# A transformer block on one core: the second feed-forward block by seven sums, the first one as jobs of the order list, key and value rows by column groups, key sums in pairs

## The chip, the cores and the metric

The kernel runs on one core of a Trainium2 chip. The metric is the device time of one execution in microseconds (us). The engines are TensorE (PE, matrix products; PEld is its weight load), VectorE (DVE), ScalarE (ACT), GpSimd (POOL) and SyncE (SP), whose queue issues nearly all DMAs. Each engine takes its instructions in the order in which the program hands them out and waits on semaphores for the others.

## The reference

```python
x = A_x                                        # 1 x 2048 x 576, bf16
sa, ca, ga, sb, cb, gb = split(silu(c) @ w_mod, 6)
h = layernorm(x) * (1 + ca) + sa
q, k, v = heads(h @ wqkv)                      # 32 heads of 18
pq, pk = q @ w_phi, k @ w_phi                  # per head
phi = concat(softmax(p), softmax(-p))          # for pq and for pk
o = (phi_q @ (phi_k^T v)) / (phi_q . sum(phi_k) + 1e-6)
x = x + ga * (o @ wo)
h = layernorm(x) * (1 + cb) + sb
x = x + gb * (relu(h @ w1) @ w2)               # 576 -> 4608 -> 576
```

## The kernel before

The 2048 tokens are 16 tiles of 128. The attention runs over all tiles first, and the feed-forward layers then run over eight blocks of two tiles (256 tokens).

**The order list.** The first part is written out by hand as the string `ORDER`, a list of jobs. A job name stands for a function, the number behind it for a tile or part, and the number after the colon for the pair of PSUM banks that its product goes to (four pairs; pair 3 is taken by the key-value sum while that runs). A job's instructions are handed out when its word comes up, so the list fixes each engine's order, but not what engines do relative to each other: there, data and buffers decide.

The jobs that the texts speak of:

- `FK`, `FQ`: the key and query weights are folded with `w_phi` on PE; `fra`/`frd` and `FQra`/`FQrd` copy the result from PSUM on ACT or DVE. `sc`, `sh`, `m2` are products for the modulation (`m2c` are the copies behind `m2`); `Z` and the spins in `sc`/`sh` are products of zeros.
- `KR`, `VR`, `QR` work out four correction rows of the folded weights. They let the layer norm's mean and shift ride along as four additional rows of x. Those rows of x come from `sa`/`sp` (statistics), `T` (transpose) and `Tc` (copy). `xd`, `xa`, `xp` scale x on DVE, ACT or POOL.
- `K`, `Q`, `V` project one tile (ten products of 288 columns, L282). `eK`/`eQ` take the exponents on ACT, `sK` and `qs` sum them on DVE, `rK` takes the reciprocals by Ln and Exp on ACT, `pA`, `pM`, `qp` scale on POOL, `vE` scales v on DVE out of PSUM. `kv` adds a tile to the key-value sum; `kv0` is the first of the sixteen, `kz` masks the result.
- `qt` transposes a query tile by DMA, `nu` is the attention product, `nO` its division on DVE, `ot`/`oc` the transpose, `W` the output product, `xr` the residual, `lb` the statistics, `ap` the normalisation, `ht`, `hd`, `ha` the transpose and modulation of block 0's input. `wo` scales the output weights on POOL.
- `td`: part of `t_part`, the differences T1 to T4 of quarters of the second feed-forward weights that the second layer works with (DVE, 128x1728 each, 12 in all).

**The feed-forward blocks.** After the list a loop runs over the eight blocks. `l2` is the second layer: seven products of quarters with sums between them, in place of eight. The first layer has two forms. `l1` is the plain one: nine groups of two column blocks, 36 products of 64 rows each, two beside each other (L732). `l1_seven` does the same by seven products out of sums, in the order written out in `SEVEN` (L781 and L798). Blocks 0 and 1 use `l1`, blocks 2 to 7 `l1_seven`:

```python
BS = 2
for b in range(NB):
    if b < BS:
        l1(b, ...)
    else:
        l1_seven(b, in_seven(b))
    l2(b, in_l2(b))
    if b + 2 < NB:
        project(2 * b + 4, WO)
```

The seven products need sums of quarters of the first layer's weights, made once by `w1_sum(k, gp)` with k from 0 to 3, for two halves gp of the columns, each 128x2048, in place. They read further quarters that `w1_more` loads. Sums k = 2 and 3 overwrite what `l1` reads. `t_feat` makes the sums of the block's input. Before, the sums lie in hooks of blocks 0 and 1: k = 0, 2, 3 on DVE and k = 1 on POOL in pieces of 512 columns:

```python
o, p, q, op = ((f[6], v[0], v[6], ALU.subtract), (f[7], v[7], f[6], ALU.subtract),
               (f[1], v[1], f[7], ALU.subtract), (f[2], v[2], v[3], ALU.add))[k]
eng.tensor_tensor(out=o, in0=p, in1=q, op=op)
```

Block 0's attention for tiles 2 and 3, the T differences and the loads also lie in hooks of blocks 0 and 1.

Of the kernel before, what the change touches and what calls it, by code (L numbers as in the profile page):

```python
# [7 lines left out]
P = 128  # L8
# [10 lines left out]
NC = 5  # L19
# [26 lines left out]
Lbdw Z11 LwkT FK Z1 fra1 Lx0 Lcc sx bn0 sd frd2 Lwsc frd0 bn1 sa0 frr sc ca Lwsh frd4 Lx2 Lid bn3 sh fra3 sp0 T0:1 shc  # L46
Lt0 KR:2 KRh0 Lwv Lx4 xd0 bn2 KRh1 mk KRd0 KRd1 Tc0 sa2 Ka0:0 VR:1 bn4 VRh0 Kb0 VRd0 sp2 VRh1 Lt1 xd2 Ka1:2 Kb1 VRd1
T2:1 eKa0 sK0 LwqT FQ3:3 Tc2 K2:0 FQra3 bn5 Lwsb eKa1 sK1 K3:3 rK0 eK2 sa4 FQ4:2 FQrd4 pM0 V0:1 sK2 Lwcb rK1 pA1 pA0
Lt2 pM1 V1:0 m2:2 eK3 FQ0:3 Lx6 vE0 V2:1 Lwga vE1 rK2 Lx10 m2c FQrd0 pA2 FQ1:3 xa4 sp4 Lt4 bn7 vE2 T4:2 Tc4 K4:0 FQra1
eK4 FQ2:2 xp6 bn6 sa6 FQrd2 sK3 Lt3 bn11 K5:1 pM2 kv0 kv1 QR:2 eK5 V3:0 kv2 QRh sp6 QRe QRd T6:2 rK3 sK4 pA3 vE3 rp  # L50
Tc6 pM3 K7:1 rK4 K6:2 pM4 pA4 eK7 eK6 Lwgb ga:0 gac V4:1 bn9 kv3 sK5 rK5 bn8 pA5 w2b0 sa8 V5:2 vE4 bn12 sp8 T8:0 xa8
pM5 vE5 Tc8 Q0:1 eQ0 gb:2 xp14 kv4 kv5 sK6 bn10 Q1:0 gbc sa10 sK7 gaw gar wl1 rK6 K8:1 qs0 wl3 bn15 eQ1 eK8 K9:2 eK9
sp10 xp10 Lwo Q2:0 pA6 sK8 pM6 eQ2 V6:1 rK8 bn13 vE6 sK9 bn14 qp0 rK7 Q3:2 pA8 T10:0 Tc10 pA7 eQ3 qs1 pM7 kv6 K10:1
eK10 rK9 K11:0 sK10 pM8 V8:2 eK11 sa14 sa12 V7:1 vE8 pM9 rK10 V9:0 vE7 xa12 sp12 pA9 kv7 T12:2 sK11 rK11 kv8 V10:1 vE9
kv9 wl0 pA10 vE10 Tc12 pM10 K12:0 sp14 T14:2 Tc14 gbw eK12 kv10 K13:1 eK13 wo2 K14:2 eK14 qt0 qs2 sK12 sK13 Q4:0 eQ4
rK13 K15:1 w2a1 qp1 V11:2 V12:0 gbr qs3 wo1 pA11 qp2 pM11 vE11 kv11 w2a2 rK12 w2a0 pA12 eK15 vE12 sK15 pM12 qt1 V13:2
kv12 pM13 Lmask sK14 Q5:1 wl4 rK15 eQ5 sq5 Q6:0 pA13 pA15 vE13 sq4 kv13 qt2 V15:2 rK14 vE15 pM15 pA14 V14:1 vE14 eQ6
Q11:2 pM14 qp3 sq6 kv14 kv15 qt3 eQ11 sq11 Q7:1 kz nu1:2 Q8:0 nu0:3 nO1 td2 eQ7 eQ8 sq7 nO0 td0 sq8 ot1:2 td1 Q9:1 oc1
Q10:0 ot0:2 wo0 wo4 eQ9 qi5 wo3 sq9 oc0 eQ10 W1:3 xr1 qi4 W0:1 lb1 Q12:2 xr0 lb0 Q13:0 lr1 eQ12 sq10 qi6 lr0 ap1 eQ13
Q14:1 ht1:2 Q15:3 ap0 wl2 ht0:0 ha eQ14 eQ15 hd w2b1 sq13 sq15 sq14 sq12  # L60
# [16 lines left out]
BS = 2  # L77
# [4 lines left out]
def tile_block(ctx, tc, a, out):  # L82
# [60 lines left out]
    m98 = carve(RS, NC * GR, (NC, NX))  # L143
    rep = carve(RS, NC * GR + NC * NX, (NC, 32))
# [13 lines left out]
    rs2 = small([P, NT, 2], FP32, "rs2")  # L158
    Rq = small([P, 2, 2 * H], FP32, "Rq")
# [90 lines left out]
    def mods(w, bank, idle=None):  # L250

        o = PS[:, bank, :] if isinstance(bank, int) else bank[:, 0, :]
        for k, wm in enumerate(w):
            for ci in range(NC):
                if idle is not None:
                    spin(1, idle)
# [16 lines left out]
    def rows_mm(raw, pr):  # L273
        for k in range(2):
            for ck in range(NC):
                pe.matmul(pr[0:NX, k, 0:HD], lhsT=m98[0:R, ck, :], rhs=raw[0:R, ck, k * HD:(k + 1) * HD],  # L276
                          start=(ck == 0), stop=(ck == NC - 1))

# [14 lines left out]

    def hs(r, s):
        return r.rearrange("p (h s) -> p h s", s=2)[:, :, s]
# [5 lines left out]
    def vv(t):  # L301
        return v_sb[:, (t + 1) % NV, :].rearrange("p (h e) -> p h e", e=VW)
# [4 lines left out]
    def k_r(t):  # L307
        Rr, r = Rk[:, t % 4, :], rk[:, t % 4, :]
# [18 lines left out]
    def kv(t):  # L327
        E = E_sb[:, t % NE, :]
        for c in range(9):
            k, o, n = kvcols(c)  # L330
            pe.matmul(PS[:, 6 + k, o:o + n], lhsT=E[:, c * P:(c + 1) * P],  # L331
                      rhs=v_sb[:, (t + 1) % NV, KVC[c][0] * VW:KVC[c][0] * VW + n],
# [23 lines left out]
    def eslot(u):  # L356
        return u % NET if u < 8 else u % 2
# [185 lines left out]
    def scale():  # L543
        dve.tensor_scalar(out=ca1[0:R, :], in0=PS[0:R, 7, 0:NC], scalar1=1.0, scalar2=None, op0=ALU.add)
        dve.tensor_scalar(out=m98[0:R, :, X0:X0 + 3], in0=ca1[0:R, :].unsqueeze(2).to_broadcast([R, NC, 3]), scalar1=-1.0,
                          scalar2=None, op0=ALU.mult)

    def x_scale(t, eng):
# [6 lines left out]
        for ck in range(NC):  # L555
# [76 lines left out]

    def stats_p(t):
        c = sc[:, t % 4:t % 4 + 2, :]
        pool.tensor_copy(c[:, :, X0:X0 + 2], mv[:, 0, t:t + 2, 0:1].to_broadcast([P, 2, 2]))
        pool.tensor_tensor(out=c[:, :, X0 + 2], in0=mv[:, 0, t:t + 2, 0], in1=c[:, :, X0], op=ALU.subtract)
        pool.tensor_scalar(out=rs[:, t:t + 2, 1], in0=rs[:, t:t + 2, 0], scalar1=-1.0, scalar2=None, op0=ALU.mult)

    def k_scale(t):
        pool.tensor_scalar(out=Ak[:, t % 4, :], in0=hs(rk[:, t % 4, :], 0), scalar1=rs[:, t, 0:1], scalar2=None, op0=ALU.mult)  # L640

    def k_minus(t):
        Rr, r = Rk[:, t % 4, :], rk[:, t % 4, :]
        pool.tensor_copy(vv(t)[:, :, DH], hs(r, 0))
        pool.tensor_tensor(out=rat[:, t % 4, :], in0=hs(Rr, 0), in1=hs(r, 1), op=ALU.mult)
# [11 lines left out]
        "sc": lambda: mods([wsc], 7, idle=6),  # L657
        "sh": lambda: mods([wsh], 7, idle=6),
        "shc": lambda: dve.tensor_copy(m98[0:R, :, X0 + 3], PS[0:R, 7, 0:NC]),
# [3 lines left out]
        "rp": lambda: pool.tensor_copy(rep[0:R], siluc[0:R, :].unsqueeze(2).to_broadcast([R, NC, 32])),  # L663
        "xd": lambda t: x_scale(t, dve), "xp": lambda t: x_scale(t, pool), "xa": lambda t: x_scale(t, act),
# [5 lines left out]
        "sK": k_sums, "rK": k_r, "pA": k_scale, "pM": k_minus,  # L670
# [17 lines left out]
        "td": lambda k: t_part(0, k, dve),  # L688
# [3 lines left out]
    for w in "KV":  # L692
        JOBS[w + "R"] = lambda w=w: rows_mm(ROWS[w], at[w + "R", None])
        for k in range(2):
            JOBS[f"{w}Rh{k}"] = lambda w=w, k=k: rows_h(at[w + "R", None], k)
# [512 lines left out]
```

## Time and profile before

| what | value |
|---|---|
| time, median of 3 runs | 374.89 us (374.74 to 375.1) |
| the profiled execution | 374.84 us, span 373.1 us |
| granted TensorE clock | 1.0 |
| busy: PE, DVE, ACT, POOL | 99%, 76%, 59%, 37% of the span |
| first key-value product (`kv0`) | 30.15 us |
| block 0's first layer from / second from | 90.7 / 112.1 us |
| block 1's first layer from / second from | 130.7 / 148.4 us |
| block 2's first layer from / second from | 167.0 / 183.2 us |

The span is what the profiler records from first to last instruction; the time holds 1.74 us more. Waits before a matrix product show as gaps in the chain of waits. A "busy" engine of DVE or POOL may contain waiting inside an instruction, which shows as an instruction that takes longer than others of its form.

### The profile page before, as it was taken

The page shows a single profiled execution, that of the slowest core. Times are in us where ns is not written, and L with a number is a line of the kernel's source. Part 1 is how long each engine was busy: PE and PEld are TensorE (multiplying, and loading weights), DVE is VectorE, ACT ScalarE, POOL GpSimd, SP SyncE. Part 2 cuts the span into 40 slices and gives each one's busy share as a digit, 9 for nine tenths or more (in the row PEclk, how much of TensorE's full clock was granted, in tenths as well). Part 3 has the DMA queues.
Part 4 walks back from the last instruction along what each step waited for, and adds up shares of the span by engine and source line. Part 5 has one row for each costly group of instructions (what it writes and reads, how often), then busy time and mean ns, then how long its engine had stood idle before and what let it go on. Part 6 is the DMA issues. An engine that isn't in the chain of part 4 may idle for free.

```text
span 373.1 us, 14298 instructions
## 1 busy us (share of the span) xinstructions
PE 367.7 (99%) x6245; PEld 313.6 (84%) x6245; DVE 282.4 (76%) x508; ACT 220.0 (59%) x495; POOL 138.9 (37%) x203
## 2 busy tenths in 40 slices
PE   8999999999999999999999999999999999999996
PEld 4787888888888788889988987898799889979975
DVE  2999998679979779987795688578668747745752
ACT  2598998588633435608752774478167608844730
POOL 2167999840302567380054007102600240044023
DMA  8985799887966436463127236512521123101001
GB/s 296 414 362 154 271 411 315 218 238 296 265 187 132 125 81 152 126 133 95 36 46 182 35 35 83 147 37 52 128 52 20 37 50 37 35 0 36 4 2 33
DMA packets 58591, 49.96 MB, mean 134 GB/s; under 512 B 46880, under 2 KB 50848, under 8 KB 57760
## 3 DMA queue, kind: packets, MB, share of 16 engines
q1 hardware_dynamic: 58384, 48.88, 48.1%
q8 instruction: 49, 0.80, 0.9%
q10 hardware_dynamic: 144, 0.16, 0.1%
q14 instruction: 14, 0.11, 0.1%
HBM read 31.98 MB, written 5.90 MB: 102 GB/s over the span
## 4 chain that ended last, share of the span: by engine, by line
PE 96%; DVE 1%; ACT 1%; issue 0%; POOL 0%; DVEq 0%; POOLq 0%
PE PS L878 33%; PE PS L798 23%; PE PS L282 15%; PE PS L732 10%; PE PS L946 4%; PE PS L781 3%; PE PS L401 2%; PE PS L331 2%; PE PS L238 1%; PE PS L276 1%; PE PS L953 1%; PE PS L418 1%; PE PS L918 1%; ACT R L558 1%; DVE RH L459 0%; DVE st L243 0%
## 5 line engine op out<-in xcount | busy, mean ns | idle before, releaser
L878 PEld LDWEIGHTS <-RH 128*128 128x128 f16 x846 | 81.7, 98 | 21.2 <-issue 0.4
L866 POOL TENSOR_TENSOR yt<-yt,gb_row 128x288 f32<-128x288 f32 x23 | 27.5, 1194 | 176.1 <-DVE yt L865 176.1
L798 PEld LDWEIGHTS <-R 64*128 64x128 bf16 (+1 forms) x1824 | 76.0, 94 | 0.8 <-issue 0.2
L878 PE MATMUL PS<-R,RH 128*128 128x288 bf16 (+1 forms) x558 | 73.2, 286 | 0.0
L798 PE MATMUL PS<-h,R 64*128 64x128 bf16 x1056 | 69.2, 216 | 0.0
L828 ACT ACTIVATE RH<-PS 128x512 f16<-128x512 f32 x96 | 50.9, 605 | 9.2 <-PE PS L798 9.0
L798 PE MATMUL PS<-RE,R 64*128 64x128 f16 x768 | 48.1, 216 | 0.0
L287 ACT ACTIVATE RT<-PS,rs 128x576 bf16<-128x576 f32 x64 | 42.9, 744 | 3.6 <-PE PS L282 3.4
L878 PE MATMUL PS<-RT,RH 128*128 128x288 f16 x288 | 37.9, 286 | 0.0
L732 PE MATMUL PS<-h,R 64*128 64x256 bf16 (+1 forms) x684 | 36.3, 264 | 0.0
L732 PEld LDWEIGHTS <-R 64*128 64x128 bf16 x684 | 31.6, 94 | 3.9 <-issue 0.2
L975 ACT ACTIVATE h<-h,mod 128x256 bf16<-128x256 bf16 x63 | 32.5, 589 | 1.0 <-DMA h<-xn 1.0
L282 PE MATMUL PS<-RH,R 116*128 116x288 bf16 x240 | 32.7, 286 | 0.1
L798 PE MATMUL PS<-h,early 64*128 64x128 bf16 x384 | 32.0, 216 | 0.0
L282 PE MATMUL PS<-RH,RT 116*128 116x288 bf16 x240 | 31.5, 286 | 0.0
L818 ACT ACTIVATE yt<-PS 128x512 f32<-128x512 f32 x10 | 6.0, 597 | 42.7 <-PE PS L798 41.8
L243 DVE BATCH_NORM_STATS2 st<-x_sb 128x6 f32<-128x288 bf16 x64 | 25.7, 443 | 6.3 <-DMA x_sb<-in_xk_dram 6.2
L865 DVE TENSOR_TENSOR yt<-PS,RS 128x288 f32<-128x288 f32 x23 | 10.5, 456 | 23.4 <-PE PS L878 23.3
L282 PEld LDWEIGHTS <-R 116*128 116x128 bf16 x240 | 22.6, 98 | 6.2 <-ACT R L626 0.4
L282 PEld LDWEIGHTS <-RT 116*128 116x128 bf16 x240 | 22.9, 98 | 5.5
L798 PEld LDWEIGHTS <-w 64*128 64x128 f16 (+1 forms) x480 | 26.4, 94 | 0.0
L867 POOL TENSOR_TENSOR x_sb<-yt,x_sb 128x288 bf16<-128x288 f32 x30 | 24.9, 833 | 3.5 <-DVE yt L863 1.7
(153 smaller groups left out, 737.9 us busy)
## 6 DMA issues: line engine op xcount, KB each, us to landing
R<-in_w_dram SPq DMA_DIRECT2D x4, 1152.0 KB
eqd<-RT SPq DMA_DIRECT2D x12, 288.0 KB, 3.6
RT<-eqd SPq DMA_DIRECT2D x12, 288.0 KB, 3.1
R<-in_w2b_dram SPq DMA_DIRECT2D x2, 1296.0 KB, 6.7
R<-in_w2a_dram SPq DMA_DIRECT2D x3, 864.0 KB
out_dram<-x_sb SPq DMA_DIRECT2D x15, 144.0 KB, 1.8
RT<-in_xT_dram SPq DMA_DIRECT2D x2, 640.0 KB, 6.5
x_sb<-in_xk_dram SPq DMA_DIRECT2D x8, 144.0 KB, 3.6
```

What stands on the lines that cost most here:

```text
L243: dve.bn_stats(out=s[:, hf, :], in_=x_sb[:, t % 8 if n else t, hf * HD:(hf + 1) * HD])
L282: pe.matmul(pr[:, k, 0:HD], lhsT=xt(t, ck), rhs=w[0:R, ck, k * HD:(k + 1) * HD], start=(ck == 0), stop=(ck == NC - 1))
L287: act.activation(out=E.rearrange("p (b h s e) -> p b h s e", b=2, s=2, e=DH)[:, :, :, s, :], in_=pr[:, :, 0:HD].rearrange("p b (h e) -> p ...
L732: pe.matmul(PS[:, 2 * u + hf, n * 256 + o:n * 256 + o + w], lhsT=w1_lhs(hf, c, j, h), rhs=hb[b0:b0 + 64, c, o:o + w], start=(n == 0 and c ...
L781: pe.matmul(PS[:, bank_at[n], j * 256:j * 256 + 256], lhsT=w1_lhs(hi, c, j, hi), rhs=hb[64 * hi:64 * hi + 64, c, :], start=(j == 0 and c = ...
L798: pe.matmul(PS[:, bank_at[BK[n] + str(g)], i * P:(i + 1) * P], lhsT=w[r, (4 * c + i) * P:(4 * c + i + 1) * P], rhs=x, start=(n in ("M1", " ...
L828: act.activation(out=o, in_=v[{"k11": "Y", "k12": "Z", "k21": "X", "k22": "W"}[n]], func=ACT.Relu)
L866: pool.tensor_tensor(out=y, in0=y, in1=gb_row[:, c], op=ALU.mult)
L867: eng.tensor_tensor(out=xs(t)[:, c], in0=y, in1=xs(t)[:, c], op=ALU.add)
L878: pe.matmul(PS[:, bank, 0:HD], lhsT=am[:, j, :], rhs=bm[:, j, :], start=first and j == 0, stop=(j % 9 == 8), skip_group_check=True)
L946: pe.matmul(pr[:, k, 0:HD], lhsT=oT[:, t % 2, ci, :], rhs=wo_sb[:, ci, k * HD:(k + 1) * HD], start=(ci == 0), stop=False, skip_group_check ...
L975: act.activation(out=o, in_=o, func=ACT.Identity, scale=mod(1, c), bias=mod(0, c))
```

## The change

- `BS` becomes 1: only block 0 uses the plain first layer, block 1 uses `l1_seven`.
- Block 0's first and second layer become jobs of the list: `lm` (a group of the first layer), `lu` (its ReLU, two on ACT and one on DVE), `lv` (U2 = U3 + A22 on DVE), `pa` (half a product of the second layer), `pc` (copy on ACT), `pf` (finish: DVE, then POOL), `px`/`py` (sums on DVE), `po` (store). So do `ou`, `wf`, `wr`, `xR` (tiles 2 and 3), the T differences `tb`, `tc`, `te` on DVE (`tep`: on POOL), the loads `wm`, and `w1_sum` as `ws` (on POOL, 2048 columns in one instruction) and `wt` (on DVE). The number behind `ws`, `wt`, `wm` is 2k + gp. In the list are `ws0` to `ws3` and `ws7`, `wt4` to `wt6`, `te1`, `te2` and `tep0`.
- The key and value rows are worked out by column groups (`quarters`, four groups of 144 columns on 32 columns of the array), as the query rows were. The value rows then go through four small DMAs, as the query rows did.
- The list sums keys in pairs: `rK`, `pA` and the new `pR` work on two tiles at once, `T`, `Tc`, `sa`, `sp` on four from tile 4 on.
- All five `FQ` copies are on ACT, x of tiles 0 and 1 is scaled by DVE (three chunks) and ACT (two), the value buffers are numbered anew, tiles 2 and 3 are normalised on ACT (`aP`), the spins within `sc` and `sh` become four ahead of `sc`. The order of loads and of the list's jobs is new throughout.

The diff, cut to its core:

```diff
@@ ORDER, from the last kv products to the end (new)
+sq4 pM15 vE15 kv14 qi5 kv15 Q6:0 qt1 kz nu1:3 eQ6 qt3 nu0:2 Q11:1 nO1 ot1:0 oc1 qt2 td0 nO0 qs5 td1 wm1 wo2 eQ11 sq6
+wo3 w2a2 Q7:3 eQ7 gbw wo1 Q9:0 wo0 W1:1 xr1 lb1 ot0:3 oc0 eQ9 Q10:2 W0:1 xr0 lb0 Q8:0 eQ10 nu2:3 nu3:1 sq9 lr1 ap1 ws1
+sq11 sq7 nO2 eQ8 lr0 Q12:2 qp5 w2b1 sq10 ws0 eQ12 sq8 Q13:0 Q14:3 ht1:2 eQ13 sq13 ou2 nO3 Q15:1 ap0 ht0:0 hd qt5 ha
+te1 td2 lm0:2 ou3 eQ14 tb2 te2 eQ15 lm4:0 qi4 lm2:3 lu0 qi8 tb1 lm1:2 lu2 tb0 sq12 ws3 wf3:3 lu4 sq14 qi6 qs4 wf2:1
+wm6 wr2 lm6:0 xR3 qp4 lu1 xR2 qs6 wm2 ws2 qp6 tep0 wm4 tc2 tc0 lm5:3 lu5 lb3 tc1 wm5 lm8:1 lu8 gbr lu6 lm3:2 lu3 lb2
+sq15 lm7:3 pa0 lv0 lr3 lu7 lr2 lv1 wt6 qt4 pa2 lv2 pa1 aP3 nu4:3 hT3 ws7 pc0 qi7 nu5:0 nO5 pa4 px aP2 pa3 pa5 py pa6
+pf0 pc1 pa7 pa8 hT2 pc2 pa9 qt6 nO4 ou4 wt4 hS2 ou5 qs7 pa10 pa11 pf1 pa12 qp7 pa13 wt5 hS1 pf2 pf3 hS0 tf0 tf2 tf1
+po0 tf3 qi9 po1 qt7
...
-BS = 2
+BS = 1
...
     def k_r(t):
-        Rr, r = Rk[:, t % 4, :], rk[:, t % 4, :]
+        Rr, r = Rk[:, t % 4:t % 4 + 2, :], rk[:, t % 4:t % 4 + 2, :]
...
-        for k in range(2):
-            JOBS[f"{w}Rh{k}"] = lambda w=w, k=k: rows_h(at[w + "R", None], k)
-            JOBS[f"{w}Rd{k}"] = lambda w=w, k=k: rows_d(at[w + "R", None], ROWS[w], k)
-    for i, w in enumerate("Q"):
+    JOBS["KR"] = lambda: quarters(at["KR", None], lambda ck: m98[0:R, ck, 28:60], wk)
+    JOBS["KRh"] = lambda: rows_h(at["KR", None])
+    for g in range(4):
+        JOBS["KRd%d" % g] = lambda g=g: rows_d(at["KR", None], wk, g)
+    for i, w in enumerate("QV"):
...
+    P2 = ((X, A11, B11, LO, 1), (X, A11, B11, HI, 0), (Y, A12, B21, LO, 1), (Y, A12, B21, HI, 0), (X, U2, T2, LO, 0),
+          (X, U2, T2, HI, 0), (Z, A11, T1, LO, 1), (X, U3, T3, LO, 0), (X, U3, T3, HI, 0), (Z, A11, T1, HI, 0),
+          (X, A22, T4, LO, 0), (X, A22, T4, HI, 0), (Z, A12, B22, LO, 0), (Z, A12, B22, HI, 0))
...
-    SUM_L1 = {(BS - 1, 7): ((2, 0),), (BS - 1, 8): ((3, 0),)}
-    for u, gp, i in ((0, 0, 0), (0, 0, 1), (2, 0, 2), (3, 0, 3), (5, 1, 0), (5, 1, 1), (6, 1, 2), (7, 1, 3)):
-        SUM_L1[BS - 1, u] = SUM_L1.get((BS - 1, u), ()) + ((1, gp, pool, 512 * i, 512),)
-    SUM_L2 = {(BS - 1, 7): (2, 1), (BS - 1, 12): (3, 1), (BS - 2, 11): (0, 0), (BS - 2, 13): (0, 1)}
...
+        "tep": lambda k: t_part(3, k, pool),
+        "ws": lambda i: w1_sum(i // 2, i % 2, pool), "wt": lambda i: w1_sum(i // 2, i % 2),
+        "wm": lambda i: w1_more(i // 2, i % 2),
...
+    held.append(7 + NL)
+    project(4, WO)
+    for b in range(1, NB):
+        l1_seven(b, in_seven(b))
         l2(b, in_l2(b))
```

More of the change, by code (lines that the diff above doesn't have):

```diff
@@ L554, in x_scale @@
             return
[L555 removed]
+        for ck in cks:
             v, f = xt(t, ck, 2), ca1[0:R, ck:ck + 1]
@@ L920, in l2, with prod2, keep, store @@
         sp.dma_start(outf[rows, HD:D], xs(t)[:, HD:D])
+    LO, HI = range(9), range(9, NK)
+    P2 = ((X, A11, B11, LO, 1), (X, A11, B11, HI, 0), (Y, A12, B21, LO, 1), (Y, A12, B21, HI, 0), (X, U2, T2, LO, 0),
+          (X, U2, T2, HI, 0), (Z, A11, T1, LO, 1), (X, U3, T3, LO, 0), (X, U3, T3, HI, 0), (Z, A11, T1, HI, 0),
+          (X, A22, T4, LO, 0), (X, A22, T4, HI, 0), (Z, A12, B22, LO, 0), (Z, A12, B22, HI, 0))
+    def prod2(i):
+        bank, am, bm, js, first = P2[i]
+        for j in js:
+            pe.matmul(PS[:, bank, 0:HD], lhsT=am[:, j, :], rhs=bm[:, j, :], start=(first == 1 and j == 0), stop=(j % 9 == 8),
+                      skip_group_check=True)
+    def keep(i):
+        act.activation(out=SS[:, i, :], in_=PS[:, X, 0:HD], func=ACT.Copy)
+    F2 = ((0, 0, Y, 0), (1, 1, Z, 2), (1, 0, X, None), (0, 1, Z, 1))
+    def store(i):
+        sp.dma_start(outf[i * P:(i + 1) * P, :], xs(i))
     NB = NT // 2
```

280 lines of the change are left out of this document (112 added, 168 removed).

## The prediction

> **What bounds the kernel now.** I read the busy times first, then the chain of waits, then the busy time by stage, and last the instructions of VectorE (DVE) and GpSimd (POOL) beside each other.
>
> ```profile
> span 373.1 us, 14298 instructions
> PE 367.7 (99%) x6245; PEld 313.6 (84%) x6245; DVE 282.4 (76%) x508; ACT 220.0 (59%) x495; POOL 138.9 (37%) x203
> ```
>
> TensorE (PE) is never without work, so a saving counts only if it takes matrix work away, and any wait that is put before a matrix instruction counts in full. The chain of waits says the same, and prices the parts that change:
>
> ```profile
> 12.89 1.43 PE PS L276 x10
> 15.30 1.23 PE PS L276 x10
> 31.01 0.43 PE PS L373 x20
> 130.66 17.69 PE PS L732 x324
> ```
>
> L276 are the key and value rows as 100-column products, L373 the same kind of rows by column groups, and L732 block 1's plain first layer. The stages (columns: PE, weight load, DVE, ACT, POOL busy):
>
> ```profile
> 30.15:75.70 45.55, 45.55 (x523) 37.05 (x521) 39.33 (x59) 38.10 (x97) 41.06 (x82) 1.00 0.84 280
> 75.70:90.68 14.98, 14.98 (x163) 12.39 (x161) 12.84 (x26) 12.59 (x25) 3.47 (x3) 1.00 0.73 239
> 90.68:112.06 21.38, 21.38 (x401) 18.26 (x402) 18.81 (x37) 11.54 (x28) 3.53 (x4) 1.00 0.91 248
> 112.06:130.66 18.60, 18.60 (x170) 14.85 (x172) 15.74 (x23) 7.42 (x18) 7.82 (x8) 1.00 0.58 129
> 166.95:183.21 16.26, 16.26 (x550) 16.04 (x544) 12.67 (x26) 12.40 (x26) 0.15 (x1) 1.00 0.25 59
> ```
>
> From 75.7 to 130.7 (end of attention, block 0) DVE is busy for 47.4 of 55.0 us and POOL for 14.8. The change makes POOL fill this gap. What two engines do to each other there shows in single instructions:
>
> ```profile
> 143.81 1.47 POOL L486 TENSOR_TENSOR w<-w,x_sb 128x512 f16<-128x512 bf16 x1
> 145.49 1.99 DVE L486 TENSOR_TENSOR R<-R,w 128x2048 f16<-128x2048 bf16 x1
> 146.36 2.13 POOL L486 TENSOR_TENSOR w<-w,x_sb 128x512 f16<-128x512 bf16 x1
> 153.72 1.35 DVE L890 TENSOR_TENSOR RH<-RH,RT 128x2304 f16<-128x2304 f16 x1
> 153.89 1.77 POOL L866 TENSOR_TENSOR yt<-yt,gb_row 128x288 f32<-128x288 f32 x1 [5.40 <-DVE yt L865]
> ```
>
> The shortest POOL L486 takes 1.147, the shortest DVE one of this form 1.161, the usual L866 in that state 0.73. At 145.49 DVE lost 0.83 until POOL's third piece ended; POOL's fourth lost 0.98 until DVE ended; at 153.89 POOL lost 1.04 until L890 ended. So a DVE operation with two inputs from SBUF and a POOL operation exclude each other, and the later one waits for the other's whole instruction. DVE operations that read PSUM, reductions and statistics run beside POOL unharmed.
>
> **The sum, part by part.** It is made against the profiled execution, 374.84 us (its span of 373.1 and 1.74 around it); the median of the runs, 374.89, is 0.05 above.
>
> *Block 1's first layer* as seven sums: 17.69 becomes the 16.26 of block 2, -1.43. Its second layer stays (18.60 in both blocks).
>
> *The opening.* Key and value rows fall from 20 products of 288 columns (2.46) to 40 of 144 (0.86). The spins fall from 22 to 15, but they stand where PE waits anyway. I walked the queues up to the first key-value product (kv0, 30.15 before). Up to the value weights the same bytes are ahead, so these land at 13.46 as before (there SyncE, SP, waited for them until then); the scaled x tiles and the four row corrections (four of about 0.36) end near 14.2, and the first exponent starts near 14.45 instead of 16.99. From there ScalarE (ACT) has hardly a gap: four exponents (1.25 each, start to start: 5.0), five query copies (0.55: 2.75; before, three were on DVE), two key-sum pairs (0.45 each), the scaling of tiles 4 and 5 (2.10), statistics and small copies (1.2), 12.0 together, so to 26.5; then the two copies behind the modulation product m2 (25.9 to 27.1), to 28.2. The last chunk of tile 4's keys needs the second of these, and kv0 follows it at 28.8, -1.35. Both orders have nine projections ahead of kv0; the new one also has the query rows (0.43) and two more transposes (0.11), so at equal work -1.9. Ends: -3.1 if a gap of ACT closes the rest of what the first exponent gains, +0.7 if the first exponent comes no earlier than 16.99. The value rows now go through four small DMAs (2.8 on SP's queue, L536), with the loads for m2 behind them; these land near 24.1, 1.7 ahead.
>
> *Keys in pairs.* 16 fewer ACT instructions of 0.26, 16 small POOL ones become longer. From kv0 to the last kv POOL is handed 39.4 us and PE 42.5 (POOL 41.06 in 45.55 before), so this is cover enough; once, at kv2, POOL's queue is late by 0.75. Before, 0.4 of waits lay in this stretch and some 0.2 follow at block 0's second tile, so +0.5. The normalisation of tiles 2 and 3 moves from DVE to ACT, which has 14 us free in block 0: nothing.
>
> *The weight sums* (k0, k1 and part of k3 on POOL, k2 and the rest on DVE) and one T3 part (tep0) on POOL. All must now be done before block 1. A POOL sum of 2048 has no row. Four rows of 512 give 4.59. The rows of 576 (1.165) and 1280 (2.318) give a fixed part of 0.22, so (1.147-0.22)x4+0.22 = 3.93. I take 4.0, as one instruction has one fixed part; tep0 likewise 3.4. POOL gets 23.4 us, room for it exists. The eight loads that feed them move earlier on SP's queue, behind the query transposes (1.3 each); the late one, gp1 of k0, lands around 4 to 8 us after the last kv product.
>
> I walked PE, DVE and POOL from the last kv product (0) to the end of block 0, first without exclusion. PE has twelve projections and output products (1.23 each), four attention products (0.38) and the transposes (1.6), so its first layer starts at 17.85; nine groups of 1.94 and the output products of tiles 2 and 3 (2.3) lead to the second layer at 37.8; 14 half products of 1.105 and two attention products end it at 54.05. DVE's list to the first layer is kz 1.1, four attention outputs of 1.1, td0 and td1 of 1.05, qs5 1.65, two residuals of 0.75, statistics and normalisation of two tiles (4.2) and the first half of hd (1.4): 16.3. To the second layer it has 20.9 us in 20, the last of it (statistics, 1.0) not yet needed there. So PE hardly waits, and DVE has about 1 us to spare. With exclusion:
> - The sum ws1 starts at 5.3, behind the scaled output weights. At 6.75 DVE reaches td1 and waits until 9.2. The residual of tile 1 behind it comes at 10.25 instead of 7.55, and tile 0's output product needs its PSUM: PE +2.3. If the load is late, td1 goes first, but then ws3 is in the way of te1 with much the same loss at lu0.
> - ws2 (31.9 to 35.9) holds tc2 from 34.0 for 1.8, qp6 falls between tc2 and tc0, tep0 holds tc1 for 3.2. Behind tc1 stand the ReLU parts that free the PSUM of the last first-layer groups: lu8 ends at 44.1, and pa0 needs that bank: 44.1 instead of 37.8 + 2.3, so +4.0.
> - ws7 holds lv0 for 1.8; pa4 waits 1.0 for U2, pa6 0.9 for px: +1.9.
>
> Sum of the exclusion +8.2. Lower end +3 (only tc1 meets a sum, less DVE's spare us), upper +12.4 (each long POOL instruction by the 4.59 row, +2.4, and ws3 in front of te1, +1.8).
>
> The rows show only instructions up to 1.3 us holding the other engine; that a 4 us one holds it to its end is drawn out from them. The Trainium skill, SBUF — State Buffer, section "Who interferes with whom", says that a VectorE instruction with two SBUF inputs and a GpSimd instruction that reads SBUF take a shared port in turn for the whole instruction, and that order of issue decides. By that rule the +8.2 stands. With waits capped at the longest that a row shows (1.04), five collisions give 5.2, of which DVE's spare time takes some 2 at the two places, so +3; this is a rival below.
>
> Total: -1.43 - 1.9 + 0.5 + 8.2 = +5.4, 380.2 us.
>
> **Rivals.**
> *The sums fall beside DVE's other work* (faster). Between td1 and te1 DVE has some 11 us of statistics, PSUM reads and reductions; if ws1, ws0 and ws3 lie there, and tep0 gets ahead of tc0, PE loses nothing. For it: POOL's 3.47 of 15 us shows how free it is. Against: ws1, qp5, ws0 and ws3 are 13.5 us, more than the gap. Decides: DVE's sum of waits staying under its spare 1 us. Time: 374.84 - 2.8 = 372.0.
> *The opening gains nothing*, because ACT is handed more before kv0 than before; the rest as forecast: 380.2 + 2.6 = 382.8. Against it: ACT is free until the first exponent.
> *The losses cancel the gains*: waits as short as the rows' longest, 374.84 - 2.8 + 3 = 375.0.
> That the change doesn't do what it says is no rival: seven-sum products of 64x128 grow from 3072 to 3584.
>
> **How the numbers follow.** A measurement here tells about 0.2% (0.75 us) from no change. Forecast 0.60, its own range 376.5 to 384.5 (from a collision fewer to the upper end); opening rival 0.10; cancelled 0.06; faster 0.24. Most of the third falls within 0.2%, so faster 0.25, same 0.04, slower 0.71. The range has to reach the faster rival: 371.6 to 384.5, leaving out part of that rival's own spread and the far end of the second.
>
> **What would show it.** Right: POOL L486 of 2048 near 4 us; DVE L512 instructions of 3 to 5 us where 1.05 is usual; PE idle of some 2 us ahead of the second output product and 4 ahead of the second layer; block 1's first layer 16.3; kv0 near 28.8. Wrong: PE dense from kv0 to block 1 (then 372), or L512 unharmed beside a running POOL sum, which would refute the exclusion for long instructions.

## The result, and the profile after

The changed kernel takes 388.22 us (median of four runs, 387.31 to 391.0) against 375.0 (374.74 to 375.21): 1.0365 times as long, 95% interval 1.0307 to 1.0424. The profiled execution is 387.31 us, its span 385.5, so 12.47 above the profiled execution before, where +5.4 was forecast (380.2) and the range ended at 384.5. The direction was right, the size was not.

The head of the page after:

```profile
span 385.5 us, 14715 instructions
PE 367.9 (95%) x6482; PEld 313.7 (81%) x6482; DVE 289.4 (75%) x500; ACT 228.0 (59%) x487; POOL 146.8 (38%) x177
```

PE is busy for as long as before (367.7), so the 12.4 us are time without matrix work, or matrix work that runs slower. The times of PE's instructions give the stages. (The first key-value product is kv0; the stage behind it ends where the last one ends, at 76.09 before and 76.08 after; every other stage ends where the next one's first product starts. Two projections, 2.45 us, moved from the key-value stage to the one behind, so these two are read together.)

| us | kv0 starts | kv0 to last kv | to first layer | to second layer | to block 1 | block 1's first layer | rest of the span |
|---|---|---|---|---|---|---|---|
| before | 30.15 | 45.94 | 14.59 | 21.38 | 18.60 | 17.69 | 224.75 |
| after | 33.21 | 42.87 | 20.98 | 22.33 | 23.11 | 17.92 | 225.08 |

From kv0 to block 1 the change costs 8.78; the forecast's parts there came to 8.2 + 0.5 - 0.54 (work moved ahead of kv0) = 8.16. The opening costs 3.06 where -1.35 was forecast, and block 1's first layer 0.23 where -1.43 was. These two are the miss: 4.4 + 1.7 of 7.0; the rest is 0.6 between and 0.3 behind.

PE's timeline after, the four longest waits behind the opening (start, duration, in brackets the idle time before and what ended it; L426 is a residual addition, L734 a ReLU part, L738 the sum U2):

```profile
87.84 1.39 PE L418 MATMUL PS<-wo_sb,oT 128*128 128x288 bf16 x10 [3.09 <-DVE x_sb L426]
117.12 2.14 PE L725 MATMUL PS<-h,R 64*128 64x256 bf16 x36 [1.70 <-DVE RH L734]
127.11 0.54 PE L908 MATMUL PS<-RT 128*128 128x288 f16 x3 [2.26 <-DVE RT L738]
144.87 0.61 PE L762 MATMUL PS<-h,R 64*128 64x256 bf16 x8 [0.87 <-DVE x_sb L426]
```

Each ends with DVE. What DVE was doing, beside POOL, in the three stretches before:

```profile
82.15 4.07 POOL L486 TENSOR_TENSOR x_sb<-R,x_sb 128x2048 f16<-128x2048 bf16 x1 [2.29 <-DMA x_sb<-in_w_dram]
83.39 3.73 DVE L512 TENSOR_TENSOR RT<-R 128x1728 f16<-128x1728 bf16 x1
111.34 4.48 POOL L486 TENSOR_TENSOR w<-w,x_sb 128x2048 f16<-128x2048 bf16 x1 [2.60 <-DMA w<-in_w_dram]
110.91 5.82 DVE L512 TENSOR_TENSOR RT<-R,RT 128x1728 f16<-128x1728 bf16 x2
122.28 4.37 POOL L486 TENSOR_TENSOR R<-R 128x2048 f16<-128x2048 bf16 x1
122.99 4.07 DVE L738 TENSOR_TENSOR RT<-RH 128x768 f16<-128x768 f16 x1
```

A POOL sum of 2048 takes 4.07, as forecast (4.0). A DVE L512 (a T part), 1.05 alone, takes 3.73 and (the second of the two at 110.91) 4.91; an L738, 0.5 alone, 4.07. Each ends within 1 us of POOL's end. It goes the other way too: at 118.05 POOL's T3 part took 4.27 (3.44 in the run with spins below), with a DVE L512 already running beside it. Statistics (0.44 to 0.46), normalisation (0.52 to 0.56) and the division out of PSUM (0.76) beside POOL's next two sums (88.44 to 96.53) kept their times, and so did the reduction beside the one at 82.15 (1.34).

The stages by busy time and granted clock (columns as in the prediction, the clock third from the end; the first row begins at 75.92, where the projection behind the last key-value product starts):

```profile
75.92:97.06 21.14, 18.05 (x193) 14.79 (x191) 19.07 (x31) 14.40 (x27) 18.24 (x9) 1.00 0.81 257
97.06:119.39 22.33, 20.50 (x383) 17.84 (x382) 21.58 (x30) 11.44 (x28) 9.39 (x6) 1.00 0.80 207
119.39:142.50 23.11, 20.58 (x167) 15.48 (x168) 21.25 (x27) 11.10 (x26) 13.70 (x10) 0.93 0.39 66
```

The last stage holds something that no line of before had shown: PE is busy 20.58 us in it, for work that took 18.51 in the run with fills below. Its clock was not full. In steps of 1.5 us, from the opening and from this stage:

```profile
10.50:12.00 1.50, 1.50 (x25) 1.41 (x24) 0.89 (x2) 1.12 (x2) 0.00 (x0) 0.83 1.05 407
16.50:18.00 1.50, 1.50 (x24) 1.00 (x25) 0.36 (x1) 0.45 (x2) 1.50 (x1) 0.50 0.95 382
18.00:19.50 1.50, 1.50 (x17) 1.16 (x15) 0.25 (x2) 1.34 (x3) 0.04 (x1) 0.89 0.20 71
128.00:129.50 1.50, 1.50 (x8) 0.97 (x7) 1.47 (x4) 0.00 (x0) 0.00 (x0) 0.50 1.15 208
```

The granted clock is a half from 11.5 to 18.3 us, and from 127.5 to 131.0 (worked out from the shares: 0.83 of 1.5 us leaves 0.5 at half). The first stretch follows these waits, and the key products in it (third line) take nearly twice their time:

```profile
8.67 0.78 PE L262 MATMUL PS<-siluc,R 116*128 116x1 bf16 x25 [2.31 <-DMA R<-in_wsc_dram]
10.40 1.72 PE L450 MATMUL PS<-RS,R 126*128 126x126 bf16 x25 [0.96 <-DMA R<-in_wkT_dram]
14.39 2.10 PE L279 MATMUL PS<-RH,R 116*128 116x288 bf16 x8
17.84 1.38 ACT L284 ACTIVATE RT<-PS,rs 128x576 bf16<-128x576 f32 x2 [0.23 <-PE PS L279]
30.36 0.78 PE L262 MATMUL PS<-siluc,RE 116*128 116x1 bf16 x25 [0.53 <-DMA RE<-in_wsb_dram]
```

Eight key products take 2.10 (1.14 before). By this, the second stretch, 3.4 us long, cost an estimated 1.7 of the 20.58. The first exponent starts at 17.84, where 14.45 was forecast and 16.99 was measured before. The 0.53 at 30.36 is a wait for the load of wsb, the weights of m2, which now stands behind the value rows' DMAs.

### The profile page after: what moved, and what is told of

It reads as the page before. It is cut to its first block, busy times and chain, and to the rows that moved or that the text cites. A ratio compares the mean times of both kernels' runs of the same rounds, so it can differ in the third digit from the quotient of the medians.

```text
span 385.5 us, 14715 instructions
## 1 busy us (share of the span) xinstructions
PE 367.9 (95%) x6482; PEld 313.7 (81%) x6482; DVE 289.4 (75%) x500; ACT 228.0 (59%) x487; POOL 146.8 (38%) x177
## 4 chain that ended last, share of the span: by engine, by line
PE 85%; DVE 6%; DMA 6%; SPq 1%; issue 0%; ACT 0%; DVEq 0%
PE PS L859 28%; PE PS L779 26%; PE PS L279 14%; PE PS L762 4%; PE PS L908 3%; DVE RT L512 3%; PE PS L943 3%; DMA RE<-in_wsb_dram 2%; DMA R<-in_wkT_dram 2%; PE PS L725 2%; DVE RT L738 2%; DMA early<-in_w_dram 1%; PE PS L331 1%; PE PS L401 1%; DVE RE L837 1%; PE PS L418 1%
## 5 line engine op out<-in xcount | busy, mean ns | idle before, releaser
L779 PEld LDWEIGHTS <-R 64*128 64x128 bf16 (+1 forms) x2128 | 88.9, 94 | 0.9 <-issue 0.2
L859 PEld LDWEIGHTS <-RH 128*128 128x128 f16 x738 | 71.3, 98 | 18.3
L779 PE MATMUL PS<-h,R 64*128 64x128 bf16 x1232 | 81.0, 216 | 0.0
L809 ACT ACTIVATE RH<-PS 128x512 f16<-128x512 f32 x112 | 59.3, 604 | 11.1 <-PE PS L779 10.9
L859 PE MATMUL PS<-R,RH 128*128 128x288 bf16 (+1 forms) x486 | 63.7, 286 | 0.0
L779 PE MATMUL PS<-RE,R 64*128 64x128 f16 x896 | 56.5, 216 | 0.0
L779 PE MATMUL PS<-h,early 64*128 64x128 bf16 x448 | 37.5, 216 | 0.0
L279 PE MATMUL PS<-RH,R 116*128 116x288 bf16 x240 | 33.5, 294 | 0.0
L279 PE MATMUL PS<-RH,RT 116*128 116x288 bf16 x240 | 31.7, 286 | 0.0
L779 PEld LDWEIGHTS <-w 64*128 64x128 f16 (+1 forms) x560 | 30.8, 94 | 0.2 <-issue 0.2
L846 DVE TENSOR_TENSOR yt<-PS,RS 128x288 f32<-128x288 f32 x23 | 10.5, 455 | 26.7 <-PE PS L859 24.8
L779 PE MATMUL PS<-RE,w 64*128 64x128 f16 x448 | 30.4, 216 | 0.0
L779 PE MATMUL PS<-RE,x_sb 64*128 64x128 f16 x448 | 29.0, 216 | 0.0
L779 PEld LDWEIGHTS <-early 64*128 64x128 bf16 x448 | 28.2, 94 | 0.4 <-issue 0.3
```

Source lines behind the costliest of these rows:

```text
L279: pe.matmul(pr[:, k, 0:HD], lhsT=xt(t, ck), rhs=w[0:R, ck, k * HD:(k + 1) * HD], start=(ck == 0), stop=(ck == NC - 1))
L779: pe.matmul(PS[:, bank_at[BK[n] + str(g)], i * P:(i + 1) * P], lhsT=w[r, (4 * c + i) * P:(4 * c + i + 1) * P], rhs=x, start=(n in ("M1", " ...
L809: act.activation(out=o, in_=v[{"k11": "Y", "k12": "Z", "k21": "X", "k22": "W"}[n]], func=ACT.Relu)
L859: pe.matmul(PS[:, bank, 0:HD], lhsT=am[:, j, :], rhs=bm[:, j, :], start=first and j == 0, stop=(j % 9 == 8), skip_group_check=True)
```

## The experiments

The theories: **A**, a POOL operation and a DVE operation with two SBUF inputs exclude each other for the whole instruction; **B**, its rival, POOL's amount of work and late loads make the waits. For the opening **C**, late key weights and the half clock took the gain; **D**, only data arrival counts, and later **F**, the opening is full anyway. **E** belongs to block 1's first layer. Times are medians, stages are those of the profiled run; "block 0" is the time from the last key-value product to block 1 (66.42 after, 54.57 before).

### Shorter POOL instructions

```diff
-"ws": lambda i: w1_sum(i // 2, i % 2, pool),
+"ws": lambda i: [w1_sum(i // 2, i % 2, pool, a, 512) for a in range(0, 2048, 512)],
```

and the T3 part as three of 576 columns.

> The changed kernel with each POOL weight sum cut into four of 512 columns, and the T3 part on POOL into three of 576; same order, same loads, POOL's work a little longer. Theory A (a two-input DVE instruction waits out the whole POOL instruction, and the other way round): a collision now costs at most 1.15 us instead of 4, so DVE's longest L512 falls from 4.9 to 2.2 or less, last key-value product to block 1 from 66.6 to about 61, the time from 387-388 to about 382.5. Theory B (POOL's amount of work and the late loads behind the sums set the waits, not the length of an instruction): POOL's sums grow by some 0.5 each, so the waits stay and the time is 388 to 390.

385.2 us; block 0 61.31. POOL was busy for 7.6 us more (154.4), and still 5.1 us of block 0 went; the longest L512 took 2.00. That is A. The total stayed above the 382.5 that A expected; in the profiled run kv0 came at 34.88 (33.21 after), with the same code, because a second half clock, from 32.1 to 35.5, followed a wait of 0.69 for wsb.

### Fills in place of the sums

```diff
-        eng.tensor_tensor(out=o, in0=p, in1=q, op=op)
+        if eng is pool:
+            pool.memset(o, 0.01)
+            pool.memset(o, 0.01)
+            return
```

> The changed kernel with each POOL weight sum, and the T3 part on POOL, replaced by two fills of the same 2048 (1728) columns with a constant: the same place in POOL's queue, the same wait for the load of the tile that is written, about the same time on POOL (two of 1.84 by the 64- and 512-column fills of the trace, 3.7 against 4.07), but nothing read. It leaves these sums out of the computation. Theory A (exclusion): no DVE L512 over 1.3 us between 75 and 143, last key-value product to block 1 falls from 66.6 to 57-58.5, block 1's first layer from 18.0 to 16.3, time 377 to 380. Theory B (POOL's load, the queue order and late loads): waits stay, 386 to 388.

381.29 us, so A's total was missed by 1.3; block 0 58.18, so 8.24 less. The opening of the profiled run ended late (kv0 35.34), with the clock at a half from 9.6 to 19.8 and from 33.5 to 36.9. One fill took 1.80, a pair 3.6. The stages:

```profile
78.50:97.17 18.67, 18.34 (x201) 14.98 (x198) 15.82 (x31) 14.26 (x27) 15.49 (x12) 1.00 0.89 257
97.17:118.61 21.44, 20.46 (x383) 17.95 (x381) 19.45 (x35) 11.32 (x27) 8.56 (x8) 1.00 1.03 253
118.61:137.12 18.51, 18.51 (x170) 14.77 (x169) 15.07 (x22) 11.22 (x26) 12.46 (x12) 1.00 0.49 82
```

With POOL nearly as occupied (36.5 us against 41.3, which held waits), its queue in the same order and the same loads ahead of it (2.9 us of wait for the first), DVE's busy time falls from 61.9 to 50.3, PE waits for 1.3 us instead of 7.5, the longest L512 takes 1.48, and the clock stays full in these stages. B is out. A DVE instruction that ran inside a fill shows it singly (POOL's fill, then DVE's; L520 is L512 here):

```profile
85.65 1.80 POOL L487 MEMSET x_sb<- 128x2048 f16 x1 [2.93 <-DMA x_sb<-in_w_dram]
86.25 0.99 DVE L520 TENSOR_TENSOR RT<-R 128x1728 f16<-128x1728 bf16 x1
```

The Trainium skill, SBUF — State Buffer, section "Who interferes with whom", says that a VectorE instruction with two SBUF inputs meets a GpSimd instruction that reads SBUF and not one that only writes it. The 0.99 beside a fill and the 3.73 beside a sum agree. Block 1's first layer, 17.78, did not fall to the 16.3 that A expected: that part has another cause.

### Spins that keep PE's clock, and the load of wsb

```diff
-... sa2 Z11 Lwsc sc sp2 bn1 ca LwkT FK ...
+... sa2 Z22 Lwsc sc sp2 bn1 ca LwkT Z4 FK ...
```

> The changed kernel with 11 more spins ahead of the first modulation product and 4 ahead of the fold, so that PE is not idle for the 2.31 and 0.96 us in which it waits there for wsc and wkT; no transfer moves. Theory C (PE came out of these waits at half its clock and lost some 2.4 us on row and key products): KR falls from 0.79 to 0.43, the 8 products of Ka1 from 2.1 to about 1.1, the first exponent from 17.84 to about 16.3, first key-value product from 33.4 to about 32 (the load of wsb, 1.4 earlier with the value rows, is next late), time about 386, and the four times lie closer together than 387.3 to 391. Theory D (only the late data count): PE rows at the old length or first key-value product at 33.2 or later, time unchanged.

387.63 us, not the 386 of C. In the opening C held: kv0 at 31.97. Further on it was given back:

```profile
14.35 1.15 PE L279 MATMUL PS<-RH,R 116*128 116x288 bf16 x8
87.28 1.62 PE L418 MATMUL PS<-wo_sb,oT 128*128 128x288 bf16 x10 [3.46 <-DVE x_sb L426]
123.00 4.84 PE L908 MATMUL PS<-R,RH 128*128 128x288 bf16 x27 [3.21 <-DVE RH L734]
```

The key products are at 1.15 again. But the two waits for POOL's sums became 3.46 and 3.21, and behind each the clock was a half (88.3 to 91.7 and 122.4 to 125.8); block 0 took 67.72. The times did not draw together either (385.54 to 388.84). Which engine comes first at a collision varies between runs: after, tc1 ran ahead of POOL's T3 part, here it waited for it (4.13), and so in the next three runs.

```diff
-FQ4:0 VRd bn4 ... eK3 sK3 Lwsb V0:2
+FQ4:0 Lwsb VRd bn4 ... eK3 sK3 V0:2
```

> The kernel of the previous run, and the load of wsb issued ahead of the four DMAs of the value rows instead of behind them. Theory C with the load next late: m2 no longer waits, first key-value product 30.4 to 31 instead of 33.4, time 384 to 385. Theory D: half a microsecond at most, 32.8 and 386.8. A third possibility: ACT's queue (nine copies and eight exponents ahead of it) is next late, first key-value product about 32, time 386.

387.56 us; kv0 31.67, so 0.3 more. That is near the third possibility of the text: m2 no longer waits (28.26), but the transposes behind it wait 0.56 for POOL's part of the statistics. Block 0 took 69.79, with a half clock from 88.1 to 91.5 and from 122.2 to 129.0.

### Block 1's first layer

```diff
-... hS1 pf2 pf3 hS0 tf0 tf2 tf1 po0 tf3 qi9 po1 ...
+... hS1 hS0 tf0 tf2 tf1 tf3 pf2 pf3 po0 qi9 po1 ...
```

> The changed kernel with the four feature sums for block 1 (t_feat, L837) ahead of the last two results of block 0 in the list (pf2, pf3) instead of behind them; nothing else. DVE stood idle for 1.68 us there, waiting for the last product. Theory E (block 1's first layer takes 17.9 instead of 16.26 because its residual addition stands on DVE behind these four sums, which begin only after block 0's last product): its first layer 16.3 to 16.6, time 1.3 to 1.6 lower than the changed kernel at the same opening. Rival: the wait only moves to the last results, or the four sums are slowed by POOL as before: 17.5 or more, no change.

386.68 us; block 1's first layer 17.26 (17.92 after), kv0 33.40. The wait of 0.87 for the residual addition is gone, as E had it, and waits of 0.32 (just ahead of this layer) and 0.38 came in its place. But this is no proof of E: runs that hold the old order here took from 17.27 (with spins and wsb, above) to 18.55 (shorter POOL instructions). With only pf3 behind the sums (the run with everything placed, below) it was 17.10. PE is busy for 16.7 to 17.04 of it in all of these runs and after, so 0.4 to 0.8 of the excess over 16.26 is no wait, and its cause stays open. Moving pf2 back as well has a price: in a later run with it (all edits) block 1's first product waited 1.12 us for the bank that pf2 still held. Block 0 took 65.31 here, 1.1 less than after, from nearly the same code, and no half clock fell into it.

### The loads as before, and the sums on VectorE

```diff
-Lbdw Lcc sx sd rp Lx0 bn0 Lx2 bn2 bn3 sa2 Z11 Lwsc sc sp2 bn1 ca LwkT FK fra0 ...
+Lbdw Z11 LwkT FK Z2 Lcc sx sd rp fra0 frd1 Lx0 bn0 Lwsc frd3 frr bn1 fra2 sa0 sp0 Z4 sc ca ...
```

> The changed kernel with the opening's loads in the order of the kernel before: the transposed key weights first and folded between spins, the modulation's weights behind them, the second block of x later. Everything from the key rows on is unchanged. Theory C (the late key weights and the half clock behind the two waits on PE made the opening lose): PE at full clock from 3 to 20 us, first exponent near 15.5 instead of 17.84, first key-value product 31 to 31.5 instead of 33.2 (the load of wsb still next late). Theory D: 33 or later. In both the time may fall by less than the opening, if a wait on PE behind it lengthens past some 3 us and halves the clock there, as in the run with spins: 384.5 to 387.

387.19 us; first exponent 16.63, kv0 32.70, the products ahead of the exponent at full clock. The exponent came 1.2 earlier and m2 1.3 (29.04), but behind m2's wait of 0.70 for wsb the clock fell to a half from 30.8 to 34.1, and 0.5 was left at kv0. Neither C nor D had that. Block 0, with the code of after, took 65.11 without a half clock: 20.03, 25.20 and 19.88 by stage, so 1.80, 3.76 and 1.37 more than with fills. Its tc1 waited for POOL's T3 part (116.73, 3.45 us), which the walk of the prediction had and the profile after had not:

```profile
116.97 4.13 DVE L512 TENSOR_TENSOR RT<-R,RT 128x1728 f16<-128x1728 bf16 x1
```

PE waited 3.21 us at the second layer here; the prediction's sign was some 4.

```diff
-wm2 ws2 qp6 tep0 wm4 ... hT3 ws7 pc0 ... pa13 wt5
+wm2 qp6 te0 wm4 ... hT3 wt7 pc0 ... pa13 wt2 wt5
```

with the other sums in pieces. (wt2 comes behind wt4 here, so one part of k2 takes an operand that is not summed yet, and the result is not that of the reference; the work is the same. So in the next run.)

> The changed kernel with the three POOL operations that met VectorE in block 0's two layers moved to VectorE (second part of k1 1.2, k3 1.2, the T3 part 1.05: 3.45 us more on DVE), at places where DVE waited for PE; the two sums of k0 and the first of k1 stay on POOL in pieces of 512. All sums are computed. Theory A (exclusion): last key-value product to block 1 falls from 66.6 to 58.5-60, no half clock there, time 7 to 8 below the changed kernel at the same opening, about 380. Rival (DVE is full, so its 3.45 us come back as waits of PE): 62 and more, 383 to 385.

382.55 us; block 0 60.19, no half clock in it. A and its rival each have a part: 6.2 of 8.2 us came back, and DVE is now busy for 56.98 of the 60.19. The time lies between what A and the rival had.

> The three edits together, with the load of wsb ahead of the value rows' DMAs as well. If they add up: first key-value product 30 to 31, last key-value product to block 1 58.5 to 60, block 1's first layer 16.4, time 374 to 376, level with the kernel before. If one of them only moves a wait: 377 to 380.

380.47 us, above both ranges: kv0 30.90, block 0 61.75, block 1's first layer 17.33.

### Everything placed

The four k0 and k1 sums whole on POOL, beside DVE work without two SBUF inputs; the T3 part and k3 on DVE, T4 parts later; the opening as in the last run, with the statistics of tiles 2 and 3 later. Two of the places:

```diff
-td0 nO0 qs5 td1 wm1
+td0 nO0 td1 qs5 wm1
-qs4 wf2:1 wm6 wr2 lm6:0 xR3 qp4 lu1 xR2 qs6 wm2 ws2 qp6 tep0 wm4 tc2 tc0 lm5:3 lu5 lb3 tc1
+qs4 wf2:1 wm2 wm6 wr2 lm6:0 xR3 qp4 ws2 lu1 xR2 qs6 lb3 qp6 wm4 lm5:3 lu5 lb2
```

> All that the runs before pointed to, with every sum computed in order. Opening: loads and spins as in the kernel before, statistics of tiles 2 and 3 behind the key rows, wsb ahead of the value rows' DMAs. Block 0: the four k0 and k1 sums whole on POOL, placed beside stretches of VectorE work without two SBUF inputs (the query sums moved behind td1; ws2 behind qp4, beside residuals, reductions and statistics); the second part of k3 and the T3 part on VectorE; four T4 and T3 parts later, the first ReLU part earlier; the feature sums for block 1 ahead of the last result only. If the exclusion can be placed around: DVE L512 at 1.05 throughout, no wait of PE over 1 us, first key-value product 29.5 to 30.5, last key-value product to block 1 58 to 59.5, block 1's first layer 16.3 to 16.8, time 373 to 376. Rival (VectorE is full with 3 us more work, so its order no longer matters): last key-value product to block 1 61 or more as in the run with all edits, time 378 to 380.

379.65 us, 1.0128 times the kernel before (1.0087 to 1.0169). No L512 took more than 2.01, and the stages to the first and second layer took 18.39 and 21.24, as with fills (18.23 and 21.44), so four POOL sums of 4.06 can be placed to cost PE next to nothing. The stage to block 1 took 21.30 instead of 18.51:

```profile
112.81:134.11 21.30, 19.00 (x168) 14.68 (x168) 21.16 (x28) 11.22 (x26) 6.97 (x9) 1.00 0.38 73
```

DVE was busy for 21.16 of it, with what had been moved there. So the rival holds for one stage. No version run here beats the kernel before.

This run also has the opening's loads and clock as the forecast took them: no half clock falls ahead of kv0. ACT's first exponent, then PE's fold of the query weights:

```profile
14.73 1.38 ACT L284 ACTIVATE RT<-PS,rs 128x576 bf16<-128x576 f32 x2 [0.47 <-PE PS L279]
17.32 0.72 PE L270 MATMUL PS<-RS,R 126*128 126x126 bf16 x12 [1.41 <-DMA R<-in_wqT_dram]
```

The first exponent is 0.28 off the forecast's 14.45, and still kv0 came at 30.12, level with the 30.15 before: PE waited 1.41 us for the query weights' load, and from 17.32 to kv0 it had hardly a gap (the longest 0.24).

### The kernel before without its spins

```diff
-"sc": lambda: mods([wsc], 7, idle=6),
+"sc": lambda: mods([wsc], 7),
```

likewise for `sh`, and Z1 taken out.

> The kernel before with its spins between and ahead of the modulation products taken out (11 of 22; the 11 ahead of the key weights stay); nothing else. They stand where PE waits for wsc, wsh and DVE. Theory C (gaps in PE's work halve its clock some us later): granted clock 0.5 for some 3 us between 10 and 18 us, row and key products longer there, first key-value product 30.5 to 32 instead of 30.15, time 375.3 to 377. Rival (the spins only take time): clock 1.0 throughout, first key-value product 29.5 to 30.15, time 374.2 to 374.9.

376.85 against 375.16 us, ratio 1.0049 (1.0030 to 1.0067). Eleven instructions that add nothing to the result were worth 1.7 us:

```profile
10.50:12.00 1.50, 1.04 (x27) 0.77 (x26) 1.39 (x6) 0.79 (x4) 0.57 (x3) 0.50 1.06 436
13.50:15.00 1.50, 1.50 (x8) 1.25 (x7) 1.35 (x4) 0.40 (x1) 0.39 (x2) 0.50 1.11 444
```

Waits of 0.84 and 1.56 between short products were enough for a half clock from 9.3 to 16.2 us; kv0 came at 31.34.

### The rows alone

The kernel before with only the rows by column groups (`quarters`, `rows_h`, `rows_d` as in the change), first with the value rows through DMAs:

```diff
-Lt0 KR:2 KRh0 Lwv Lx4 xd0 bn2 KRh1 mk KRd0 KRd1 Tc0 sa2 Ka0:0 VR:1 bn4 VRh0 Kb0 VRd0 sp2 VRh1 ...
+Lt0 KR:2 KRh Lwv Lx4 xd0 mk KRd0 KRd1 KRd2 KRd3 Tc0 Ka0:0 VR:1 bn2 VRh Kb0 VRe sa2 sp2 bn4 ...
+LwqT Lwsb Lwcb Lt2 Lx6 VRd T2:1 eKa0 ...
```

> One part of the change alone: the kernel before with its key and value rows by column groups (40 products of 144 columns in place of 20 of 288; four corrections of the key rows on VectorE, value rows through four DMAs), loads, spins and everything else as in the kernel before, the DMAs behind the loads in SP's queue. Theory C (the change's opening was right in its -1.9 for the rows, and lost it to the loads' new order and the half clock): clock 1.0, first exponent 15 to 15.6 instead of 16.99, first key-value product 28.3 to 29 instead of 30.15, time 373.0 to 374.2 against 375.1. Rival (ACT's queue of exponents, copies and scaling is full from its start, or the value rows' DMAs are late for the first value product): first key-value product 29.8 or later, 374.7 to 375.5.

378.36 us, slower than both expected, ratio 1.0088 (1.0066 to 1.0110). The four small DMAs were issued at 16.34 (third column the queue, then PE's wait for them):

```profile
16.34 2.80 SPq L534 DMA_DIRECT2D RH<-yt  x4
24.36 3.14 PE L282 MATMUL PS<-RH,R 116*128 116x288 bf16 x12 [1.90 <-DMA RH<-yt]
```

They carry 1.1 KB each, and the last landed at about 24.3, while the DMA engines moved 416 GB/s of loads. Behind this wait the clock was a half from 24.8 to 31.7, and kv0 came at 34.70. This edit had also put a statistics job ahead of the first exponent, which came at 16.48. The next takes both away:

```diff
-VRe ... VRd
+VRd0 VRd1 VRd2 VRd3   (on VectorE, as for the key rows)
```

> As the run before (the kernel before with key and value rows by column groups), but the value rows are corrected on VectorE like the key rows (four of 0.36), so no DMA of theirs queues behind 10 MB of loads; the statistics of tiles 2 and 3 stand behind the first exponent on ACT, and the query weights are loaded ahead of tile 4's rows. Theory C: first exponent 15.2 to 15.6 instead of 16.99, first key-value product 28.6 to 29.4 instead of 30.15, time 373.6 to 374.4 against 375.1. Theory F (the opening's loads, 10.46 MB at 370 to 400 GB/s, arrive when they did and set the pace from 18 us on, so a shorter row product only waits for them): first exponent early too, but the query fold or the second modulation product waits, first key-value product 29.8 to 30.3, 374.7 to 375.3.

376.1 us (1.0018 to 1.0050 times before), slower than both expected. Its times fall by the clock: the six runs at 0.999 or 1.0 lie from 375.69 to 376.7, the three at 0.991 to 0.995 from 377.18 to 378.26. Even at full clock it gained nothing. With four more spins, so that the profile shows the full clock:

> The run before (rows by column groups alone, corrected on VectorE, in the kernel before) with four more spins between the key fold and the first modulation product, where PE waited 1.1 us for wsc and its clock fell behind that in part of the runs. Theory C: clock 1.0 in every run, first exponent 15.2 to 15.6, first key-value product 29 to 29.5, time 374.0 to 374.6. Theory F (from 18 us on the loads, VectorE or ACT's queue set the pace whatever the rows take): clock 1.0, first exponent early, but the products behind it wait; first key-value product 30 to 30.5, time 375.2 to 376, as in the undisturbed half of the run before.

376.98 us, 1.0055 times before (1.0041 to 1.0068), clock 1.0 in every run; F had 376 at most. ACT, then PE twice:

```profile
15.48 1.38 ACT L287 ACTIVATE RT<-PS,rs 128x576 bf16<-128x576 f32 x2 [0.55 <-PE PS L282]
17.73 0.27 PE L621 MATMUL PS<-ident,early 128*128 128x128 bf16 x2 [1.12 <-DVE RH L519]
30.57 0.86 PE L331 MATMUL PS<-RT 128*128 128x76 bf16 x18
```

The first exponent is 1.51 earlier than in the kernel before, as C had it, and kv0 0.42 later. F: DVE has no gap of over 0.25 us from 8.4 to 33, and the corrections of the key and value rows, eight parts of 0.36, take it 3.0 us, where four of 0.52 took 2.0 in the kernel before; PE waits for them at 17.73, and ACT for 1.55 behind that for the scaled x tiles. That DVE's queue is what holds kv0 here is read from these waits; no run took work off DVE in the opening. A wait of 0.85 for a weight load in a first layer adds to the total.

## Why the prediction was right and wrong

**The exclusion** (+8.2) was right in mechanism: taking the reads away gave 8.24. That the size agrees so closely is in part luck. By stage the forecast had 2.3, 4.0 and 1.9; after against fills has 2.75, 0.89 and 4.60. The first collision was the one forecast (ws1 and td1; PE waited 3.09). At the second, tc0 lost 3.9 to ws2 and lv0 1.3 to the T3 part, while tc1 came first and lost nothing; at the third lv1, not lv0, met ws7 and lost 3.5, and PE waited 2.26 instead of 1.0. Some 6.1 of the 8.24 are waits of PE (7.45 against 1.31); about 1.7 are the half clock behind the last one, which the sum did not have. The walk itself fits better where tc1 did meet the T3 part and no half clock followed: the run with the loads as before has 1.80, 3.76 and 1.37, together 6.9. That a 4 us instruction holds the other engine to its end, drawn out of 1 us rows, is now shown by rows.

**The opening** (-1.9 at equal work) is the step that failed: +2.5. The forecast walked one queue, ACT's, up to kv0, and put what PE waits for ahead of it and beside it at nothing: the spins "stand where PE waits anyway", and the loads carry "the same bytes". After shows what that left out. The key fold waited for its weights until 10.40 (5.96 before), since they now load behind others. PE's clock was a half from 11.5 to 18.3, so the first exponent came at 17.84 instead of 14.45. And 15.4 us lay between it and kv0, with a wait of PE for wsb among them, where 14.35 was forecast (14.40 was reached once, in the run with all edits, from a first exponent at 16.50). Such idle-time spins are not nothing: 11 of them were worth 1.7 us in the kernel before, and 15 more took 1.24 off kv0 in the changed one. With the loads and spins of before, and wsb and the statistics moved, kv0 came at 30.12 and the whole loss was gone.

The gain of 1.35 did not come even then. In that run the first exponent was at 14.73, close to the forecast, but kv0 was where it had been before: PE waited 1.41 for the query weights, a wait that the walk did not have. In the rows alone, where these weights load earlier, the corrections on DVE came late instead. So, as the traces read, the saving of 1.6 us in PE work went into waits, for a load in the one case and for DVE in the other; no run took both away at once. The upper end, +0.7, assumed that nothing new could be late.

**Block 1's first layer** (-1.43): +0.23. Reading block 2's 16.26 over was wrong: after, PE waits 0.87 there for a residual addition that stands on DVE behind the four feature sums, and is busy for 17.04 instead of 16.26. Why the same products keep PE busy for 0.8 longer stays open, and so does how much of the wait the order of the sums costs.

**Keys in pairs and the waits behind them** (+0.5) cost nothing that shows. Without two projections (2.45), the query rows and two transposes (0.54), the 45.94 before would be 42.95; after has 42.87. The prediction's 0.4 of waits before is in no row either: its own line has PE busy for 45.55 of 45.55.

**The rivals.** None came as written. The second had it that the opening gains nothing; it even lost time, and the waits shown above are PE's for loads and DVE, not more work for ACT. That the sums can fall beside DVE's other work was a real possibility, as the run with everything placed shows for four of them, and the order in the list was not that one.

## What to carry to other kernels

When work moves to an idle GpSimd, look at which of its operations read SBUF and which VectorE operations with two SBUF inputs stand beside them: in these runs it cost next to nothing beside PSUM reads, reductions and statistics, and up to a whole 4 us instruction otherwise. Before booking a gain on one engine's queue, list every engine and the landing of every load for that stretch; where several are nearly full, a shorter step on one may only make it wait for another. Count a wait on TensorE at its length plus what it may do to the clock, and do not remove idle-time matrix instructions before looking at the granted clock.

## What the runs showed of the hardware that was not expected

A half clock of PE behind waits far shorter than a stage: after 2.31 and 0.96 us (after), 2.26 (after, 127 us), 3.46 and 3.21 (with spins), 0.84 and 1.56 (before without spins), and even 0.64 (fills, 31.7 us), 0.69 (shorter POOL instructions, 30.8 us) and 0.70 (loads as before, 29.0 us). The last three stand just ahead of m2's products, which are one column wide. Each stretch lasted 3.4, 6.8 or, once, 10.2 us. The length of the wait does not decide it: 3.09 up to 87.8 us (after) and 3.21 up to 121.5 us (loads as before) had none behind them. The Trainium skill, TensorE: Matmul & The Clock Gate, section "Part 1: The HAM clock gate (the "warmup" mystery)", puts this down to free-running windows of about 3.4 us, with half rate after an idle one. The half rate and the stretches of one to three such windows agree. An idle window was not needed here: in the 3.4 us ahead of 127.5 PE worked for a third, in those ahead of 11.5 for over half. What does decide it, these runs do not show.
